# Attention and a bilinear feed-forward on one core: queries and keys by transposing DMAs, and the second tile's outputs by seven products

## The chip, the cores and the metric

The kernel runs on one core of a Trainium2 chip. The metric is the device time of one execution in microseconds (us), the median of three runs. A core has five engines that this text names as the profile does: PE (TensorE, matrix products; its weight loads are listed as PEld), DVE (VectorE), ACT (ScalarE), POOL (GpSimd) and SP (SyncE). Sixteen DMA engines move data between DRAM and on-chip memory. Here POOL issues the loads from DRAM (queue 0 in the profile) and SP the stores and on-chip copies (queue 1).

## The reference

Eight batches of attention with 8 heads, 576 positions and 64 features per head; then a feed-forward over all 4608 positions. The first four heads of a batch see only the last 32 positions ("local"), the last four only positions of the same remainder modulo 32 ("strided").

```python
def _attn_ref(q, k, v):
    scores = scale * np.matmul(q, k.transpose(0, 1, 3, 2))
    rel = pos[:, None] - pos[None, :]
    mask_local = (rel >= 0) & (rel < stride)                       # stride = 32
    mask_strided = (rel >= 0) & (pos[None, :] % stride == pos[:, None] % stride)
    ...
    attn = np.exp(scores)
    attn = attn / (np.sum(attn, axis=-1, keepdims=True) + 1e-09)
    return np.matmul(attn, v)

def _moe_ref(x, w_a, w_b, w_out):
    a = x @ w_a
    b = x @ w_b
    return a * b @ w_out
```

x is the attention's output with the heads side by side, 4608 x 512; w_a and w_b are 512 x 1536, w_out is 1536 x 512. All inputs and the output are float32 in DRAM; the kernel computes in bf16 with float32 sums.

## The kernel before, in words

**Work and order.** The feed-forward is cut into 9 tiles of 512 positions (t = 0 to 8). A tile has 16 slots: 12 slots `ffn_ab` (L629), each with the products of one block of 128 columns of w_a and w_b (eight matmuls of 512 columns, L626), a copy of the first result by ACT (L647) and the multiplication by DVE (L650, L652) into `pf`; then 4 slots for the outputs. Slot i of tile t is number 16 t + i. The attention of batch b is cut into small steps that are put between the matmuls of tile b - 1 by tables (`STEPS`, `LATER`, `IN_Y`, L584 to L592): S0 to S7 are scores (matmuls L392, exponential by ACT L413, mask by DVE L431), V0 to V7 the products with the values. A step at a half number lies in the middle of a slot. Every engine runs its instructions in the order in which the program records them, and waits at each for what it needs.

**An attention unit V** of the third batch (b = 2), and V4 to V7 of the later ones, is `step_VT` (L518): matmuls into the one bank pair `o` (L529), on ACT a logarithm and an exponential (L538, L539) that make reciprocals, and two multiplications by DVE (L543, L545) into `xT`, which free `o`.

**Outputs of a tile** come in two ways. The plain product, `ffn_y` (L886), has 48 matmuls of 512 columns (L892), four ACT copies (L901) and four stores. Tiles in `FAST_Y` use seven products in place of eight quarter products, `y_plan` (L815): sums of `pf` blocks are made before by DVE in `fast_s` (L754, L764) and of weights in `fast_w` (L172); then 7 x 2 x 6 = 84 matmuls of 256 columns (L830) go into three banks X, Y and Z in the order 1, 7, 6, 4, 5, 2, 3 (`Y_ORDER`, L803). Each bank collects several products, and each product's end is copied by ACT or added by DVE (`y_post`, L789, L795, L797, L799, L801) before the next product adds into the same bank. 21 matmuls make a slot, and a step in the middle of a slot comes after the 11th. Before the change `FAST_Y` holds tiles 2 to 8; tiles 0 and 1 use the plain product.

**Queries and keys of a batch.** The scores need keys (`kT_buf`) and queries (`qz_buf`) with the features on the partitions; the queries of two heads stand there twice, each time with the other head's half zero. Batches 0 and 1 are transposed by PE (`T_p`, L279). From the third batch on (`FIRST_D` = 2), `load_qk` (L187) brings keys and queries by POOL into on-chip tiles (`kl`, `ql` at L212, `natk`, `natq` at L203), `step_D` (L320) transposes blocks of 32 x 32 with DVE (L329, L334), and SP copies the pieces into place, 8 key copies (L346) and 16 query copies (L350) per batch. The zeros in the queries are written once (`zero_qz`, L114, and `rezero`, L355, on POOL at slot 14).

**What sets the times.** `do(i, ...)` (L1008) hangs loads, transposes and stores on slots. From slot 14 on, POOL first copies one element that the slot has produced (`pace`, L1076), so its loads are issued no earlier than that slot. SP has no such pace: a DMA on it starts as soon as the ones before it are issued and what it waits for is there. Local rows also use a transposing DMA already: `rows_out` (L508) writes the attention's result to DRAM (`xd`) and `rows_in` (L514, L516) reads it back transposed into `xT`, 576 rows of 128 columns at a time.

**The start.** SP loads the first heads (`raw`, L934 to L936) and POOL all the rest; the weights come in pieces (`load_w`, L249), then `wo_sb`, then the third batch's queries and keys at slots 0 and 1 of the program's order.

Of the kernel before, what the change touches and what calls it, by code (L numbers as in the profile page):

```python
# [8 lines left out]
BF16 = mybir.dt.bfloat16  # L9
# [5 lines left out]
FIRST_D = 2  # L15
RL = 6
RS = 8
NP = 72
GP = 80
NY = 18  # L20
YS = 24
# [5 lines left out]
FAST_Y = (2, 3, 4, 5, 6, 7, 8)  # L27
# [4 lines left out]
def kernel(  # L32
# [46 lines left out]
    qz_buf = [[tuple(t[:, j] for t in pair) for j in range(2)] for pair in qz_pair]  # L79
# [4 lines left out]
    nat_s = {nm: const.tile([128, 3, RS * D], BF16, name=f"nat{nm}") for nm in "qk"}  # L84
# [27 lines left out]
    spare = qz_buf[0][0][0][:, 0]  # L112

    def zero_qz(i, eng, parts=((0, 0), (0, 1), (1, 0), (1, 1))):  # L114
        for j, z in parts:
            t = qz_buf[i][j][z]
            if (i, j, z) == (0, 0, 0):
                t = t[:, 1]
            if eng is nc.scalar:
                nc.scalar.copy(t, spare[:, :1].unsqueeze(2).to_broadcast(list(t.shape)))  # L120
            else:
                eng.memset(t, 0.0)

# [63 lines left out]
    def load_qk(b, strided, heads=range(HL), names="kq"):  # L187
        for nm in names:
            src = {"k": k, "q": q}[nm]
            if b < FIRST_D:  # L190
                n, R, h0 = (NP, RS, HL) if strided else (96, RL, 0)
                w0 = {"k6": 0, "q6": 1536, "k8": 3072, "q8": 5120}[f"{nm}{R}"]
                if b not in shared:
                    shared[b] = nat.tile([128, FG * 5 * SW], BF16, tag="shared", name="shared")
                t = nats[b, nm, strided] = shared[b][:n, w0:w0 + HL * R * D].rearrange("p (h r d) -> p h r d", r=R, d=D)
                hs = slice(heads[0], heads[-1] + 1)
                nc.gpsimd.dma_start(out=t[:, hs], in_=src[b, h0:h0 + HL].rearrange("h (p r) d -> p h r d", r=R)[:, hs])  # L197
            elif strided:

                t = nat_s[nm]  # L200
                n = 32 if b == FIRST_D else YS
                for h in heads:
                    nc.gpsimd.dma_start(  # L203
                        out=t[32 * h:32 * h + n],
                        in_=bass.AP(tensor=src.tensor, offset=(b * H + HL + h) * S * D,
                                    ap=[[RS * D, n], [YS * RS * D, 3], [1, RS * D]]))
            else:
                if 0 in heads:
                    nats[b, nm, strided] = nat.tile([128, NY, D], BF16, tag=f"{nm}l", name=f"{nm}l")
                t = nats[b, nm, strided]  # L210
                for h in heads:
                    nc.gpsimd.dma_start(out=t[32 * h:32 * h + 32],  # L212
                                        in_=src[b, h].rearrange("(i y) d -> y i d", y=32))
            nats[b, nm, strided] = t
# [105 lines left out]
    def step_D(b, z, nm, part):  # L320
        src = nats.get((b, nm, z == 1))
        if part == 0:
            tl[b, z, nm] = blocks(nm, z)
        t = tl.get((b, z, nm))
        if part is None:
            last = True
        elif z == 0:
            i = slice(NY // 2 * part, NY // 2 * (part + 1))
            nc.vector.transpose(t.rearrange("p h (i y) -> p i h y", i=NY)[:, i],  # L329
                                src[:, i].rearrange("p i (h d) -> p i h d", h=2))  # L330
            last = part == 1
        else:

            nc.vector.transpose(  # L334
                t.rearrange("p h (r c) -> p r h c", r=RS)[:, :, :, YS * part:YS * part + 32],
                src[:, part].rearrange("p (r h d) -> p r h d", r=RS, h=2))
            last = part == 2
        if last:
            for nm, c in {"k": (("k", 0),), "q": (("q", 0), ("k", 1), ("q", 1)), "r": (("k", 1), ("q", 1))}[nm]:
                if part is not None and z == 1 and c == 1 and b > FIRST_D:  # L340
                    continue
                t = tl[b, z, nm]
                for e in range(2):
                    if nm == "k":
                        dst = kT_buf[b % 2][z][64 * e:64 * e + 64, c]
                        nc.sync.dma_start(out=dst[:, PAD:] if z == 0 else dst[:, :RS * GP], in_=t[64 * c:64 * c + 64, e])  # L346
                        continue
                    for j in range(2):
                        r0 = 64 * c + 32 * j
                        nc.sync.dma_start(out=qz_buf[b % 2][j][z][64 * e + 32 * j:64 * e + 32 * j + 32, c],  # L350
                                          in_=t[r0:r0 + 32, e])
                if (nm, c, z) == ("q", 0, 0) and b - 1 > FIRST_D:
                    rows_in(b - 1, 1)

    def rezero(b):  # L355

        for j in range(2):
            for t in qz_buf[b % 2][j]:
                nc.gpsimd.memset(t[32:64] if j == 0 else t[64:96], 0.0)
# [22 lines left out]
    def S_p(b, u):  # L382
        c, half, M, n, G = unit(u)
        kT = kT_buf[b % 2][c // 2]

        st = pst.tile([128, 2, 512], F32, tag="st", name="st")
        held[b, "st", u] = st
        if b > 0:
            sv = st.rearrange("p a (i n) -> p (a i) n", n=256)
            for i in range(G):  # L390
                k0 = (G * half + i) * (LW if c < 2 else GP)
                nc.tensor.matmul(sv[:, i, :2 * n].rearrange("p (j n) -> p j n", j=2), lhsT=kT[:, c % 2, k0:k0 + 128],  # L392
                                 rhs=qz_pair[b % 2][c // 2][:, :, c % 2, k0:k0 + n], start=True, stop=True)
            return
        qz = tl[0, c // 2, "q"]
        if b == 0 and c >= 2:
            for j in range(2):
                r = slice(64 * j, 64 * j + 64)
                nc.tensor.matmul(st[:, j, :W], lhsT=nm_l[r], rhs=nm_r[r].unsqueeze(1).to_broadcast([64, G, n]),
                                 start=True, stop=False)  # L400
        for i in range(G):
            k0 = (G * half + i) * (LW if c < 2 else GP)
            for j in range(2):
                d = slice(64 * j, 64 * j + 64)
                nc.tensor.matmul(st[:, j, i * n:(i + 1) * n], lhsT=kT[d, c % 2, k0:k0 + 128],
                                 rhs=qz[d, c % 2, k0:k0 + n], start=c < 2, stop=c < 2 or i == G - 1)
# [161 lines left out]
    def step_X(b, c):  # L568
# [16 lines left out]
                 10: "V6 Tk0", 10.5: "Tq0 Pk1 Z0", 11: "Pq1", 12: "V7 Tk1 S0 W0 W1", 12.5: "Tq1 W2",  # L585
                 12.6: "S1", 12.75: "L0 X2", 13: "s2 X3 V0 m2 L1 W3", 13.5: "V1 S3", 14: "V2 X0", 14.5: "V3 D1", 15: "X1"},
             2: {20: "S0", 20.5: "S1", 21.5: "V0", 22: "S2", 23: "V1", 23.5: "S3", 24.5: "V2", 25: "S4", 26: "V3", 26.5: "S5",
                 27.5: "V4", 28: "S6", 28.5: "V5", 29: "S7", 29.5: "V6", 30.5: "V7"}}
    LATER = {-1: "S0", 0: "S1", 1: "V0", 2: "S2", 3: "V1 O0", 4: "S3 I0", 5: "V2", 6: "S4", 7: "V3 O1", 8: "S5", 9: "V4",
# [5 lines left out]
          "Z": lambda b, n: zero_qz(0, nc.vector, ((1, 1),)), "D": lambda b, n: step_D(FIRST_D, 0, "k", n)}  # L595
# [325 lines left out]
    with tc.manual_schedule(engines={ENG.PE, ENG.SP, ENG.Pool, ENG.DVE, ENG.Activation}):  # L921
# [20 lines left out]
        zero_qz(1, nc.scalar, ((0, 1),))  # L942
# [9 lines left out]
        for nm in ORDER:  # L952
# [24 lines left out]
            elif nm == "Z":  # L977
                zero_qz(1, nc.scalar, ((0, 0),))
# [25 lines left out]
        steps[16 * (B - 2) + 9][-1][1].append("I1")  # L1004
# [16 lines left out]
        for b in range(FIRST_D, B):  # L1021
# [7 lines left out]
            else:  # L1029
                for h in range(HL):  # L1030
                    do(g0 + h + (2 if b == FIRST_D + 1 else -2), load_qk, b, False, (h,))
                    do(g0 + h + (6 if b == FIRST_D + 1 else 2), load_qk, b, True, (h,))
                    do(g0 + h + 10, load_vs, b, (h,))
                do(g0 + (10 if b == FIRST_D + 1 else 7), load_vl, b)
            gs = {2: (14, 14, 15, 15, 16, 16, 17, 17, 18, 18), 3: (8, 9, 10, 11, 12, 13, 14, 15, 16, 17)}.get(b) or (
                3, 5, 7, 9, 12, 13, 14, 15, 16, 17)
            for (z, nm, part), g in zip(((0, "k", 0), (0, "k", 1), (0, "q", 0), (0, "q", 1), (1, "k", 0), (1, "k", 1),
                                         (1, "k", 2), (1, "q", 0), (1, "q", 1), (1, "q", 2)), gs):
                if (b, z, nm, part) != (FIRST_D, 0, "k", 1):
                    do(g0 + g, step_D, b, z, nm, part)  # L1040
            if b > FIRST_D:
                do(g0 + 19, step_D, b, 1, "r", None)
# [9 lines left out]
        do(1, zero_qz, 1, nc.vector, ((1, 1),))  # L1052
        do(4, zero_qz, 1, nc.vector, ((1, 0),))
        for i, jz in ((2, (0, 0)), (3, (1, 0)), (0, (0, 1))):
            do(i, zero_qz, 0, nc.vector, (jz,))
        do(14, rezero, 1)
# [53 lines left out]
```

## Time and profile before

| what | value |
|---|---|
| median of 3 runs | 325.23 us (325.07 to 325.52) |
| span of the profiled execution, first to last instruction | 324.3 us |
| mean granted clock of PE | 0.999 |
| share of the chain that ended last: PE, DMA, POOL | 88%, 5%, 4% |
| DMA packets, amount | 110725, 40.44 MB |

The profile shows one execution. Its parts are: the busy time of each engine, the span in 40 slices, the DMA queues, the chain of work that ended last (followed back from the last instruction to what released it), the costliest groups of instructions, and the DMA issues. In a group's line stand the source line, engine and operation, output and input with their shapes, the count, the busy time and the mean of one in ns, and then the idle time of the engine before them with what ended it. In a timeline a line is: start, length, engine, source line, operation, shapes, count. Matmuls overlap in the pipeline, so their listed lengths (379 ns for 512 columns) are longer than the distance from one start to the next. The records of single DMA packets give start, length, size and queue.

### The profile page before, as it was taken

The numbers are of one execution on the slowest core, as the hardware profiler recorded it, in microseconds if no ns is written. First come the engines' busy times: TensorE is split into PE (matmuls) and PEld (weight loads), VectorE is DVE, ScalarE is ACT, GpSimd is POOL, SyncE is SP. The second block draws the span as 40 slices with busy tenths as digits, with TensorE's granted clock in tenths as the row PEclk, the third lists the DMA queues.
The fourth block names the chain that finished last, engine by engine and source line by source line (L and its number), as shares of the span: only waits on it lengthen the run. The fifth ranks groups of instructions, "written<-read, shape, count | busy, mean of one in ns | idle before, by whom it ended". The sixth has DMA issues, their size and how long they took to land.

```text
span 324.3 us, 7477 instructions
## 1 busy us (share of the span) xinstructions
PE 316.7 (98%) x2669; PEld 211.2 (65%) x2698; DVE 259.9 (80%) x563; ACT 190.9 (59%) x338; POOL 162.7 (50%) x293
## 2 busy tenths in 40 slices
PE   8999999999999999999999999999999999999994
PEld 7764555455555577556999895559555866786684
DVE  6766797888878988898889888988999667857862
ACT  6762776468674576447654765467546655535541
POOL 8844938689948534762576338734004003202520
PEclk9999999999999999999999999999999999999999
DMA  8999999899999999999899999999137030004004
GB/s 154 138 203 195 203 191 173 169 173 143 133 224 124 147 88 99 107 187 179 94 111 183 183 108 92 158 205 131 30 81 166 20 115 18 0 2 129 1 3 129
DMA packets 110725, 40.44 MB, mean 125 GB/s; under 512 B 88672, under 2 KB 107744, under 8 KB 110688
## 3 DMA queue, kind: packets, MB, share of 16 engines
q0 software_dynamic: 85968, 19.48, 66.0%
q1 hardware_dynamic: 24576, 20.42, 24.9%
q8 instruction: 21, 0.34, 0.4%
q14 instruction: 16, 0.13, 0.1%
q10 hardware_dynamic: 144, 0.07, 0.1%
HBM read 39.51 MB, written 10.91 MB: 155 GB/s over the span
## 4 chain that ended last, share of the span: by engine, by line
PE 88%; DMA 5%; POOL 4%; DVE 1%; issue 1%; ACT 1%; POOLq 0%
PE mm L626 42%; PE mm L830 17%; PE mm L892 6%; PE mm L710 5%; DMA wb_sb<-in_moe_w_b_dram 5%; PE st L392 4%; PE ax L703 3%; PE mm L703 2%; PE o L529 2%; PE o L470 2%; PE mm L857 2%; POOL shared L197 1%; PE end L857 1%; POOL wa_sb L252 1%; POOL vl L225 1%
## 5 line engine op out<-in xcount | busy, mean ns | idle before, releaser
L626 PE MATMUL mm<-xT,wb_sb 128*128 128x512 bf16 (+1 forms) x381 | 88.2, 352 | 0.7 <-DMA wb_sb<-in_moe_w_b_dram 0.4
L626 PE MATMUL mm<-xT,wa_sb 128*128 128x512 bf16 (+1 forms) x367 | 86.6, 351 | 0.8
L647 ACT COPY a_sb<-mm 128x512 f32<-128x512 f32 x84 | 49.2, 586 | 47.6 <-PE mm L626 45.6
L626 PEld LDWEIGHTS <-wb_sb 128*128 128x128 bf16 x392 | 37.8, 98 | 34.3 <-DMA wb_sb<-in_moe_w_b_dram 1.1
L1076 POOL CAST pace<-pf 1x1 f32<-1x1 bf16 x82 | 24.5, 298 | 64.3 <-DVE pf L650 42.7
L626 PEld LDWEIGHTS <-wa_sb 128*128 128x128 bf16 x392 | 35.1, 98 | 21.1
L650 DVE TENSOR_TENSOR pf<-a_sb,mm 128x512 bf16<-128x512 f32 x62 | 42.1, 679 | 7.3 <-PE mm L626 6.1
L413 ACT ACTIVATE p<-st 72x576 bf16<-72x576 f32 (+1 forms) x56 | 36.4, 650 | 14.4 <-PE st L392 14.2
L545 DVE TENSOR_TENSOR xT<-o,xr 64x288 bf16<-64x288 f32 x48 | 21.4, 446 | 14.8 <-ACT xr L539 14.5
L830 PEld LDWEIGHTS <-ps 128*128 128x128 bf16 x288 | 28.0, 98 | 3.1
L795 ACT COPY y_sb<-mm 128x512 f32<-128x512 f32 (+1 forms) x28 | 15.6, 556 | 17.6 <-PE mm L830 15.0
L830 PE MATMUL mm<-wf,ps 128*128 128x256 bf16 x216 | 25.5, 273 | 0.0
L710 PE MATMUL mm<-xT,wb_sb 128*128 128x512 bf16 x83 | 25.3, 379 | 0.1
L538 ACT ACTIVATE xr<-o 64x576 f32<-64x576 f32 x28 | 18.1, 648 | 12.1 <-PE o L529 11.9
L892 PE MATMUL mm<-wo_sb,pf 128*128 128x512 bf16 x93 | 23.1, 379 | 0.2
L243 POOL DMA_DIRECT2D vs<-in_v_dram x24 | 19.7, 820 | 4.8 <-PE mm L830 2.4
L830 PEld LDWEIGHTS <-pf 128*128 128x128 bf16 x216 | 20.3, 98 | 2.5 <-issue 0.2
L1076 POOL COPY pace<-y_sb 1x1 f32<-1x1 f32 x23 | 4.6, 200 | 33.1 <-DVE y_sb L793 20.1
L539 ACT ACTIVATE xr<-xr 64x576 f32<-64x576 f32 x28 | 19.1, 683 | 0.9
L652 DVE TENSOR_TENSOR pf<-a_sb,mm 128x512 bf16<-128x512 f32 x22 | 14.9, 677 | 4.8 <-ACT a_sb L647 2.7
L212 POOL DMA_DIRECT2D kl<-in_k_dram x24 | 16.0, 667 | 5.2 <-issue 2.9
L830 PE MATMUL mm<-wo_sb,pf 128*128 128x256 bf16 x144 | 18.5, 273 | 0.1
(189 smaller groups left out, 598.0 us busy)
## 6 DMA issues: line engine op xcount, KB each, us to landing
out_dram<-y_sb SPq DMA_DIRECT2D x12, 512.0 KB, 4.8
out_dram<-y_sb SPq DMA_DIRECT2D x11, 256.0 KB, 3.9
vl<-in_v_dram POOLq DMA_DIRECT2D x6, 384.0 KB, 7.8
kl<-in_k_dram POOLq DMA_DIRECT2D x24, 72.0 KB, 3.1
ql<-in_q_dram POOLq DMA_DIRECT2D x24, 72.0 KB, 3.2
vs<-in_v_dram POOLq DMA_DIRECT2D x24, 72.0 KB, 4.3
wo_sb<-in_moe_w_out_dram POOLq DMA_DIRECT2D x4, 384.0 KB, 9.5
natk<-in_k_dram POOLq DMA_DIRECT2D x20, 72.0 KB, 3.6
```

The source lines that it names most:

```text
L243: nc.gpsimd.dma_start(out=vs_buf[b % 2][:, h, :, 0:D], in_=v[b, HL + h].rearrange("(p r) d -> p r d", r=RS))
L413: nc.scalar.activation(p_flat(p)[:M, :2 * W].rearrange("p (i n) -> p i n", n=2 * n), st[:M].rearrange("p a (i n) -> p (a i) n", n=256)[:, ...
L538: nc.scalar.activation(r, sums, ACT.Ln)
L539: nc.scalar.activation(r, r, ACT.Exp, scale=-1.0)
L545: nc.vector.tensor_mul(dst.rearrange("d (p r) -> d p r", r=RS)[:, :, G * half:G * (half + 1)], o[:64, j, :W].rearrange("d (g p) -> d p g", ...
L626: nc.tensor.matmul(ps_[:, c0:c0 + n], lhsT=w[:, kk, 128 * f:128 * (f + 1)], rhs=xT[:, kk, x0:x0 + n], start=(kk == first and c0 == 0), sto ...
L647: nc.scalar.copy(a_sb, ab[0])
L650: nc.vector.tensor_mul(pf[:, f, :].rearrange("p (i a s) -> p a i s", i=2, s=16), halves(a_sb), halves(ab[1]))
L710: nc.tensor.matmul(got[e], lhsT=wb_sb[:, kk, 128 * f:128 * (f + 1)], rhs=xT[:, kk, x0:x0 + TTOK], start=kk == 0, stop=kk == KD - 1)
L830: nc.tensor.matmul(bank[b][:, q], lhsT=lhs(g, q), rhs=rhs(g), start=k in "172" and q == 0 and g == 0, stop=g == FG - 1, skip_group_check=True)
L892: nc.tensor.matmul(ybank[j], lhsT=pf[:, f, 128 * j:128 * (j + 1)], rhs=wo_sb[:, f], start=(f == 0), stop=(f == FD - 1))
L1076: nc.gpsimd.tensor_copy(pace, done)
```

## The change

Three things change together.

- From the third batch on, `load_qk` writes keys and queries, converted to bf16, into DRAM tiles (`kr0`/`kr1` for keys with two buffers each, `q_rows` for queries with one each), and `step_D` reads them with transposing DMAs on SP: per batch and kind of head one for the keys (576 rows of 256 columns) and four for the queries (576 rows of 128 columns). DVE's transposes and the 24 copies per batch are gone.
- The zeros stand in the DRAM rows beside each query: `zero_rows` writes them once for each kind, by SP from a tile `spare`. `rezero` on POOL and part of `zero_qz` are gone. The order of the recorded program leaves the two zeroing DMAs with one wait, for DVE's first memset, and directly behind the three `raw` loads on SP.
- `FAST_Y` takes tile 1 in, so its outputs are made by `y_plan`, with `fast_s` on DVE before.

The core of the diff:

```diff
-FAST_Y = (2, 3, 4, 5, 6, 7, 8)
+FAST_Y = (1, 2, 3, 4, 5, 6, 7, 8)
...
-    qz_buf = [[tuple(t[:, j] for t in pair) for j in range(2)] for pair in qz_pair]
+    qz_buf = [[tuple(t[:, :, j] for t in pair) for j in range(2)] for pair in qz_pair]
+    q_rows = [dram.tile([S, HL, 2, D], BF16, name=f"qr{z}", tag=f"qr{z}", bufs=1) for z in range(2)]
...
-    spare = qz_buf[0][0][0][:, 0]
+    spare = const.tile([96, FD * D], BF16, name="spare")
...
+    def zero_rows(z):
+        nc.sync.dma_start(out=q_rows[z].rearrange("(p g) (c j) e d -> p (g c) (j e d)", g=6, j=2)[:, :, D:2 * D],
+                          in_=spare.rearrange("p (n d) -> p n d", d=D))
...
+            if (b, nm, strided) not in nats:
+                nats[b, nm, strided] = q_rows[strided] if nm == "q" else dram.tile([S, HL, D], BF16, tag=f"kr{strided}",
+                                                                                  name=f"kr{strided}")
+            rows = nats[b, nm, strided]
+            if nm == "q":
+                rows = rows[:, :, 0]
+            if strided:
+
                 for h in heads:
+                    nc.gpsimd.dma_start(out=rows[:, h].rearrange("(r p) d -> p r d", r=RS),
+                                        in_=src[b, HL + h].rearrange("(p r) d -> p r d", r=RS))
             else:
+                nc.gpsimd.dma_start(out=rows, in_=src[b, :HL].rearrange("h t d -> t h d"))
...
+    def step_D(b, z, nm, c=None):
+
+        rows = nats[b, nm, z == 1]
+        if nm == "k":
+            t = kT_buf[b % 2][z]
+            nc.sync.dma_start(out=t[:, :, PAD:] if z == 0 else t[:, :, :S], in_=rows.rearrange("t h d -> t (h d)"),
+                              transpose=True)
+            return
+        flat = rows.rearrange("t h e d -> t (h e d)")
         for j in range(2):
+            nc.sync.dma_start(out=qz_pair[b % 2][z][:, c, j, :S], in_=flat[:, 256 * c + D * j:256 * c + D * j + 128],
+                              transpose=True)
...
+                do(18 if b == FIRST_D + 1 else g0 - 2, load_qk, b, False)
                 for h in range(HL):
-                    do(g0 + h + (2 if b == FIRST_D + 1 else -2), load_qk, b, False, (h,))
                     do(g0 + h + (6 if b == FIRST_D + 1 else 2), load_qk, b, True, (h,))
...
+            gs = {2: (15, 15, 15, 18, 18, 18), 3: (9, 10, 11, 14, 15, 16)}.get(b) or (5, 6, 7, 10, 11, 12)
+            for (z, nm, c), g in zip(((0, "k", 0), (0, "q", 0), (0, "q", 1), (1, "k", 0), (1, "q", 0), (1, "q", 1)), gs):
+                do(g0 + g, step_D, b, z, nm, c)
...
-        do(14, rezero, 1)
+        do(10, zero_rows, 0)
+        do(11, zero_rows, 1)
```

In the last lines g0 is 16 (b - 2). The strided scores of the later batches now step by 72 columns instead of 80, and the second half of the local result (`rows_in(b, 1)`) is issued from the table `LATER` at position 9 instead of from `step_D`.

## The prediction

> **What bounds the kernel now.** I read the page first (busy shares and chain), then PE's waits, then the timelines at the three places that the change touches. Busy shares and the chain:
>
> ```profile
> PE 316.7 (98%) x2669; PEld 211.2 (65%) x2698; DVE 259.9 (80%) x563; ACT 190.9 (59%) x338; POOL 162.7 (50%) x293
> ...
> PE 88%; DMA 5%; POOL 4%; DVE 1%; issue 1%; ACT 1%; POOLq 0%
> ```
>
> PE is busy in 98% of the span and makes 88% of the chain. All that PE waited for by name, in the whole execution:
>
> ```profile
> PE misc L155 <- PEq L1094: 0.9, 1, 0.9
> PE mm L626 <- DMA wb_sb<-in_moe_w_b_dram: 0.4, 1, 0.4
> PE tp L296 <- DMA shared<-in_q_dram: 0.3, 1, 0.3
> ```
>
> Nothing is on this list after 29.1 us, where the third piece of `wb_sb` lands. From 57 to 317 us the matmul starts follow each other at 216 ns for 512 columns (8 in 1.73 us in the chain) and 109 ns for 256 (12 in 1.31 us); the few larger gaps, about 0.2 us each, are single records missing from the trace. So after 57 us every matmul taken away is a gain, every stall put in is a loss, and DVE's 80% costs nothing today.
>
> **The change part by part.** The sum is made against the profiled span, 324.3 us; the median of the runs, 325.2, lies 0.9 above it, and I keep that.
>
> 1. *Second tile, plain product to seven products.* Out go 48 matmuls of 512 columns: 48 x 0.2163 = 10.38 us. In come 7 x 2 x 6 = 84 of 256 columns: 84 x 0.1092 = 9.17 us. All lie on PE: **-1.21**.
>
> 2. *What the seven products wait for there.* In the third tile the phase begins with this on ACT:
>
> ```profile
> 117.01 0.65 ACT L538 ACTIVATE xr<-o 64x576 f32<-64x576 f32 x1 [0.54 <-PE o L529]
> 117.69 0.68 ACT L539 ACTIVATE xr<-xr 64x576 f32<-64x576 f32 x1
> 118.40 0.59 ACT L795 COPY y_sb<-mm 128x512 f32<-128x512 f32 x1
> 118.88 0.65 ACT L413 ACTIVATE p<-st 72x576 bf16<-72x576 f32 x1
> 119.88 0.59 ACT L795 COPY y_sb<-mm 128x512 f32<-128x512 f32 x1 [0.35 <-PE mm L830]
> ```
>
> The reader is to see that an attention unit V puts two ACT instructions (its logarithm starts 0.46 us after V does, then 0.65 + 0.68) ahead of the copy of product 1, and that product 6 adds into the bank that this copy reads. In the third tile one V stands ahead of the phase and two lie late in it. In the second tile four lie inside (V4 to V7 at positions 27.5, 28.5, 29.5, 30.5), with the scores S6 and S7. Counted from the first product matmul: V4 comes after 11 matmuls, at 1.20; ACT is through its pair at 3.03 and through copy 1 at 3.64. PE has product 1, V4 (0.25), product 7 and S6 (0.25) done at 3.12, so product 6 waits 0.5. The same count carried on: copy 6 stands behind V5's pair and ends at 6.94 where product 5 could start at 6.76 (0.2); copy 5 stands behind V6's pair and holds product 3 (0.14); V7 needs the bank that V6's two DVE multiplications free (0.1). Behind a waiting matmul everything on PE queues. Together **+0.9**, bounds 0 (copies always in time) and 1.5 (every V a full 0.5 late).
>
> 3. *The transposes leave DVE.* 60 stream transposes go (24 of 0.77, 36 of 0.70 us: 43.7 us), and POOL's four memsets at L359 (4.4 us). DVE gets ten sums for tile 1 (nine of 0.4, one of 0.66) and three additions of 0.68: +6.3. PE waits for DVE nowhere today: **0**.
>
> 4. *Zero rows.* Two new DMAs stand on SP behind the first three loads and wait only for DVE's first memset, over at 1.25 us, so they issue at about 2.2 us, not at slots 10 and 11 where the code has them. They write 2 x 1152 pieces of 128 bytes, 144 per DMA engine. Nothing like them is in the trace. The packet records give neighbours with 256-byte pieces: a transpose alone runs at 17.5 ns apiece per engine (458 starts in 0.5 us at 252.0), a write to DRAM at 24 (333 in 0.5 us at 111.5). So 2.5 to 3.5 us of every engine, from 4.6 us on, shared with the loads. Those set the start:
>
> ```profile
> 14.49 14.60 DMA wb_sb<-in_moe_w_b_dram
> 29.09 0.05 issue
> 29.14 1.90 PE mm L626 x8
> ```
>
> PE already stands still for 0.4 us before 29.14, so what delays this landing shows in full. Between 9 and 15 us POOL's issues, 0.7 to 0.8 us each, leave the engines about a fifth free, some 2 us, which hides most. I take **+0.5**; bounds 0 and 2.5.
>
> 5. *Third batch, the first through DRAM.* Its loads keep their place on POOL behind the weights. Local keys and queries keep 2304 descriptors each; strided ones go from 768 packets of 1024 bytes to 4608 of 128. Back to back the records show 600 starts of 128-byte packets per 0.5 us (at 48 us) against 100 of 1024 (at 43 us), so 3.8 us either way; they are in by about 58. SP then stands where it stands today:
>
> ```profile
> 57.90 1.77 SPq L346 DMA_DIRECT2D kT0l<-tk  x2
> 59.78 0.53 SPq L903 DMA_DIRECT2D out_dram<-y_sb  x1
> 60.40 2.48 SPq L350 DMA_DIRECT2D qz0l<-tq  x4
> ```
>
> The fourth store now issues at 58.25 (its copy ends then), the key transposes at 58.8. One 576x128 piece costs SP 1.15 us when nothing holds it and lands 2.4 us after its issue begins (both from the existing transpose at L516; behind a large store it issued in 2.84). Keys are two pieces, the first chunk's queries two: issued by 63.4, landed by 64.7, or 65.6 behind the store. The first score needs them here:
>
> ```profile
> 66.36 0.41 PE L392 MATMUL st<-qz0l,kT0l 128*128 128x192 bf16 x3
> ...
> 69.48 0.42 PE L529 MATMUL o<-p,vl 128*128 128x96 bf16 x6
> ```
>
> About 1 us is left. The values `vl` that the second row needs (issued 61.34, landed 67.8 today) now share the engines with transposes that take 36 x 17.5 = 630 ns of each 1150: 192 packets per engine at 13.3 ns become some 5.7 us instead of 3.5, landing near 70. **+0.35**; bounds 0 and 2. POOL's second load of queries waits, the buffer being single, until the third batch's query transposes have read it, near 68; behind it stand the pace copies and `vs`, which V4 needs at 82.3 and which still issues by 76: 0.
>
> 6. *Later batches.* Per batch SP issues 12 pieces x 1.15 = 13.8 us against 24 copies x 0.59 = 14.2, in a tile of 34 us. Engine time: 12 x 0.63 = 7.6 us in, 24 copies (1024 packets at 60 ns, 3.8 us) out, strided loads 3.8 for 2.9: today's packets of a tile at these prices come to about 20 us, after it to 25, of 34. The local keys are issued at slots 5 to 7 of a tile for scores at slot 15, the strided at 10 to 12 for 22: **0**.
>
> Sum: -1.21 + 0.9 + 0.5 + 0.35 = +0.55, so 325.2 + 0.55 = **325.8**. Less than 0.2% (0.65 us), about what a measurement of this kernel can tell from no change, lies between 324.6 and 325.9; the forecast is at the upper edge.
>
> Two rules of the Trainium skill speak against the change. "VectorE: DVE Perf Modes" (The three transpose paths) gives a 128x128 block 311 ns on VectorE and 1309 by DMA; by it a piece of 4.5 blocks would be an estimated 5.9 us, 12 of them 71 us in a tile of 34, and the sum would be some 180 us worse. The trace shows 1.15 us per piece, so I give that little weight. "DMA: Bandwidth & Descriptors" (Specifications) says that below 512 bytes a transfer is a read-modify-write; the 256-byte writes at 24 ns against 17.5 fit a small surcharge, and no run here shows 128-byte ones.
>
> **The rivals.**
> - *The gain comes through.* ACT's copies are in time or the zero rows fit in the gaps: at least 0.65 of the 1.75 us of costs is absent. For it: PE waits for ACT nowhere today. Against it: ACT's program order in the second tile. 324.0 to 324.7. Chance 0.16.
> - *The third batch comes late: slower.* Place: first score at 66.36. If a 128-byte packet into DRAM costs 26 ns instead of 13.3, 9216 of them take 15 us, not 7.7: the strided queries land at 65 and `vl`, in the same queue behind them, near 71.5; with pieces held to 1.8 us, between 1.15 and 2.84, four issue by 66 and land at 67.3. PE then stands 2 us in place of 0.35; with -1.21 + 0.9 + 0.5 of parts 1, 2 and 4 that is 325.2 + 2.2 = 327.4. It decides once keys and queries land more than 1 us later than counted. For it: a margin of 1 us. Against it: queue 0 is nearly empty at 58 us. Chance 0.22.
> - *SP becomes the bound: slower.* If every later piece issues in 2.84 us, 12 make 34 us, with 4.3 for the other issues 38 in a tile of 34: 4.5 us x 5 tiles, 348. Against it: that row stands only behind 512 KB stores. This is where the first rule above would lead, only further. Chance 0.06.
>
> **How the numbers follow.** Forecast 0.52, its own range 325.0 to 326.6: 0.32 within 0.2%, 0.20 slower. First rival 0.13 faster, 0.03 within. The other two 0.28 slower. The last 0.04 I halve between faster and slower. Faster 0.15, same 0.35, slower 0.50. The range 324.4 to 328.2 leaves out the best end of the first rival and SP as the bound.
>
> **What would show it.** Part 1: 84 rows of 256 columns at tile 1. Part 2: gaps before product 6 of 0.5 us with ACT's copy as releaser. Part 4: two issues at 2.2 us on SP, and `wb_sb`'s landing later than 29.1. Part 5: a wait of L364 or L501 for DMA near 66 to 70. Wrong would be waits for transposes after 100 us, or no gap in tile 1.

## The result, and the profile after

The changed kernel takes **330.22 us** (median of four runs, 327.28 to 331.36), the kernel before beside it 325.38 us (325.07 to 325.77). The ratio is 1.0136, with a 95% interval of 1.009 to 1.0183: slower by about 4.5 us, where I had forecast 325.8 and a range up to 328.2. Its runs lie 4 us apart, those of the kernel before 0.7 us. The comparisons below leave out executions that were slow at a lower granted clock; of the changed kernel's repetition, after_again, that leaves one of four.

The profiled execution took 330.83 us with a span of 329.1 us, 4.8 us over that of before. The page of the changed kernel, busy shares and chain:

```profile
PE 317.7 (97%) x2734; PEld 214.6 (65%) x2734; DVE 230.5 (70%) x513; ACT 191.5 (58%) x339; POOL 154.6 (47%) x236
...
PE 77%; DMA 15%; ACT 3%; POOL 2%; DVE 1%; issue 1%; POOLq 0%; ACTq 0%
```

DVE is busy for 29 us less; its records, which overlap, are 36 us shorter in sum, where 37 were counted. But the DMA share of the chain goes from 5% to 15%. What PE waited for in the changed kernel (total us, times, longest):

```profile
PE mm L598 <- DMA xT<-xd: 3.2, 2, 1.8
PE o L442 <- DMA vl<-in_v_dram: 0.9, 2, 0.5
...
PE mm L802 <- ACT y_sb L767: 0.4, 1, 0.4
```

The first line is new. L598 is the feed-forward's matmul (L626 before), and it waits for `xT<-xd`: the transposing DMA of `rows_in` (L488, was L516), a part of the kernel whose amount of work the change leaves as it was (it moves only the place from which the second half's read-back is issued). The chain of waits of the changed kernel at that place:

```profile
183.21 8.25 DMA xd<-xl
191.48 6.66 DMA xT<-xd
198.18 1.02 PE mm L598 x4
```

The local result of two heads is written to DRAM (8.25 us to land), read back transposed (6.66 us), and PE stands still until 198.18. In the kernel before the same two steps took 6.53 and 4.87 us and ended 2.3 us before PE needed them. Where the 4.8 us went, from the starts of the matmul records at the first product of each tile:

| stretch | before, us | after, us | difference |
|---|---|---|---|
| start to second tile | 57.70 | 58.50 | +0.80 |
| second tile | 35.63 | 35.30 | -0.33 |
| third and fourth tile | 67.34 | 67.63 | +0.29 (a gap of 0.30 at 128.1, at the same matmul) |
| fifth tile | 34.18 | 33.91 | -0.27 (a gap at 184 us of before is absent) |
| sixth tile | 33.67 | 35.65 | **+1.98** (the wait above) |
| seventh tile | 33.42 | 34.97 | **+1.55** (the same wait at 231.6) |
| eighth tile to last matmul | 57.80 | 57.80 | 0 |
| last matmul to end | 4.60 | 5.37 | +0.77 (the last store landed 3.5 us after its issue instead of 2.5) |

The last row I take for chance: among all the profiles below that store lands now after 2.5, now after 3.5 us. The rest is two facts: a start 0.8 us later, and 3.8 us of waits for the row outputs.

The DMA side shows them coming. From the stages 162 to 196 us of the kernel before and of the changed one (after the length of the stage: busy time of PE, PEld, DVE, ACT, POOL, then the granted clock, DMA share, GB/s; the share is the sum of packet times over 16 engines' time, so packets in flight together count twice):

```profile
162.00:196.00 34.00, 33.84 (x355) 30.21 (x354) 29.40 (x61) 20.18 (x33) 18.70 (x36) 1.00 1.10 141
```

```profile
162.00:196.00 34.00, 34.00 (x361) 30.52 (x359) 24.05 (x51) 20.27 (x34) 18.35 (x28) 1.00 1.82 150
```

1.10 became 1.82, with hardly more bytes per second. The share does not say how full the engines are: back to back, 128-byte loads alone show 2.46 (changed kernel, 49 us), transposes alone 1.05 (kernel before, 252 us). The packet records of these stages: 9924 of 128 bytes before, 14592 after; 2304 of 256 bytes before (the expectation of packed_loads has 1152), some 8300 to 10000 after in the three later stages.

The packet records show one thing more. Twice in the trip above the engines of the changed kernel move next to nothing, for 1.2 us in the write and for 1.4 us in the read-back (the last two numbers are the DMA share and GB/s):

```profile
184.10:185.30 1.20, 1.20 (x19) 1.10 (x18) 1.17 (x4) 0.59 (x1) 0.37 (x1) 1.00 0.70 12
195.90:196.60 0.70, 0.47 (x3) 0.10 (x1) 0.60 (x2) 0.54 (x1) 0.19 (x1) 1.00 0.00 0
196.60:197.30 0.70, 0.00 (x0) 0.00 (x0) 0.33 (x1) 0.00 (x0) 0.00 (x0) 1.00 0.09 9
```

Just ahead of each, at 183.6 and 195.0 us, a packet of 16 KB starts on queue 8 (instructions) and takes 1.0 and 1.7 us; in the kernel before such a packet, at 184.0, passes while the engines move 192 GB/s. Packets of up to 512 bytes that take over 0.7 us number 366 in the changed kernel and 161 to 419 in the other kernels below that send keys or queries through DRAM, but 23 in the kernel before and 26 in seven_only, which send neither. These stops last 2.6 us in the two legs, which together are 3.5 us longer than before. They are not the whole: in no_q_transposes the same two legs are 0.9 and 0.5 us longer than before without one. No run takes the stops away and leaves the transfers, so what makes them and what they cost is not shown.

### The profile page after: what moved, and what is told of

Its sections match the earlier page's. It is cut to its first block, busy times and chain, and to the rows that moved or that the text cites. A ratio compares the mean times of both kernels' runs of the same rounds, so it can differ in the third digit from the quotient of the medians.

```text
span 329.1 us, 7287 instructions
## 1 busy us (share of the span) xinstructions
PE 317.7 (97%) x2734; PEld 214.6 (65%) x2734; DVE 230.5 (70%) x513; ACT 191.5 (58%) x339; POOL 154.6 (47%) x236
## 4 chain that ended last, share of the span: by engine, by line
PE 77%; DMA 15%; ACT 3%; POOL 2%; DVE 1%; issue 1%; POOLq 0%; ACTq 0%
PE mm L598 40%; PE mm L802 11%; DMA xd<-xl 7%; DMA xT<-xd 6%; PE mm L682 6%; PE st L364 3%; PE mm L864 3%; PE ax L675 3%; PE o L442 2%; DMA vl<-in_v_dram 2%; PE mm L675 2%; PE mm L829 2%; PE o L501 2%; POOL shared L199 1%; PE end L829 1%
## 5 line engine op out<-in xcount | busy, mean ns | idle before, releaser
L598 PE MATMUL mm<-xT,wa_sb 128*128 128x512 bf16 (+1 forms) x384 | 88.5, 352 | 3.3 <-DMA xT<-xd 3.2
L598 PE MATMUL mm<-xT,wb_sb 128*128 128x512 bf16 (+1 forms) x384 | 88.5, 352 | 0.0
L622 DVE TENSOR_TENSOR pf<-a_sb,mm 128x512 bf16<-128x512 f32 x74 | 50.7, 685 | 29.7 <-PE mm L598 18.8
L598 PEld LDWEIGHTS <-wb_sb 128*128 128x128 bf16 x392 | 37.9, 98 | 37.7 <-issue 4.6
L1041 POOL CAST pace<-pf 1x1 f32<-1x1 bf16 x72 | 24.1, 335 | 75.6 <-DVE pf L622 60.5
L598 PEld LDWEIGHTS <-wa_sb 128*128 128x128 bf16 x392 | 35.1, 98 | 21.2
L802 PEld LDWEIGHTS <-ps 128*128 128x128 bf16 x336 | 32.4, 98 | 4.5 <-issue 1.0
L802 PE MATMUL mm<-wf,ps 128*128 128x256 bf16 x252 | 30.4, 273 | 0.5 <-ACT y_sb L767 0.4
L767 ACT COPY y_sb<-mm 128x512 f32<-128x512 f32 (+1 forms) x32 | 17.9, 560 | 17.5 <-PE mm L802 14.7
L802 PEld LDWEIGHTS <-pf 128*128 128x128 bf16 x252 | 23.7, 98 | 2.9
L211 POOL DMA_DIRECT2D krTrue<-in_k_dram x24 | 20.6, 901 | 3.6 <-issue 2.0
L211 POOL DMA_DIRECT2D qr<-in_q_dram x24 | 19.5, 813 | 5.4 <-DMA wo_sb<-in_moe_w_out_dram 1.2
L802 PE MATMUL mm<-wo_sb,pf 128*128 128x256 bf16 x168 | 21.7, 273 | 0.0
L736 DVE TENSOR_TENSOR ps<-pf 128x512 bf16<-128x512 bf16 (+1 forms) x49 | 19.7, 402 | 0.8
```

The lines of the kernel that those rows point to most:

```text
L211: nc.gpsimd.dma_start(out=rows[:, h].rearrange("(r p) d -> p r d", r=RS), in_=src[b, HL + h].rearrange("(p r) d -> p r d", r=RS))
L598: nc.tensor.matmul(ps_[:, c0:c0 + n], lhsT=w[:, kk, 128 * f:128 * (f + 1)], rhs=xT[:, kk, x0:x0 + n], start=(kk == first and c0 == 0), sto ...
L622: nc.vector.tensor_mul(pf[:, f, :].rearrange("p (i a s) -> p a i s", i=2, s=16), halves(a_sb), halves(ab[1]))
L736: nc.vector.tensor_tensor(s[:, n], a, b, op=op)
L802: nc.tensor.matmul(bank[b][:, q], lhsT=lhs(g, q), rhs=rhs(g), start=k in "172" and q == 0 and g == 0, stop=g == FG - 1, skip_group_check=True)
L1041: nc.gpsimd.tensor_copy(pace, done)
```

## The experiments

"Waits" are gaps between matmul starts in the profiled execution, beyond the length of the matmul.

### The change taken apart

**seven_only**: only the second tile's seven products, in the kernel before.

```diff
-FAST_Y = (2, 3, 4, 5, 6, 7, 8)
+FAST_Y = (1, 2, 3, 4, 5, 6, 7, 8)
```

> The kernel before, with the second tile's outputs by seven products and nothing else: VectorE's stream transposes and the copies on SP stay. The two parts of my sum that belong here are -1.21 us of matmuls and +0.9 us of waits for ACT (1.05 us in the profile of the changed kernel), so 0.2 to 0.3 us faster than before, about 325.1, with PE gaps near 85, 88 and 91.5 us. A rival: VectorE, which keeps the transposes here, cannot take the second tile's sums and additions in time, and the phase stalls for DVE: then 326 or more.

Measured 327.05 us, ratio 1.005 (1.0033 to 1.0067): slower by 1.6 us, the rival. PE in the second tile (L529 is V):

```profile
82.42 0.42 PE L529 MATMUL o<-p,vs 72*128 72x72 bf16 x8 [0.33 <-DVE xT L543]
...
86.82 0.37 PE L529 MATMUL o<-p,vs 72*128 72x72 bf16 x6 [0.88 <-DVE xT L545]
```

The four gaps of part 2 are there as counted (0.55, 0.23, 0.15, 0.13), and two more for DVE (0.49 and 1.04): with the transposes still on it DVE is busy for 31.4 of the 34 us from 58 to 92 (24.1 in the changed kernel) and frees the bank too late. So the two halves of the change belong together: the way through DRAM is what makes the second tile's products worth 0.3 us instead of costing 1.

**path_only**: the other part alone, `FAST_Y` without tile 1.

> The changed kernel with the second tile by the plain product again, so only the way through DRAM and the transposing DMAs is left. If the loss is all in that way (row outputs late at two or three tiles, zero rows at the start), this is as slow as the changed kernel or 0.2 us slower: 330.0 to 330.5, and PE again waits for the row outputs' transposes near 196 and 231 us. If the second tile's seven products shift the later tiles into the collision, the waits go and it comes near 326.5.

Ratio 1.0076 (1.0054 to 1.0099; 327.8 and 328.6 us). One wait for the row outputs, 2.3 us at 229; that at 196 was absent. The waits belong to the way through DRAM, and which tile they hit changes from run to run.

**keys_only**: keys through DRAM, queries by DVE as before, second tile by seven products.

> One part of the change alone: keys through DRAM and transposing DMAs, queries by VectorE's transposes and copies as before, the second tile by seven products. DMA share per tile between 1.1 and 1.7, near 1.35. If lateness needs nearly full engines, the row outputs are in time and there is no wait after 100 us; the start has no zero rows (0.4 us less); VectorE has half its relief, so the second tile's two waits for DVE (1.5 us where VectorE keeps all transposes) are between 0 and 1.0: 325.2 to 326.5 by this. If instead the order on SP is the cause, the row outputs wait for the key pieces and it is 327 or more.

325.88 us, ratio 1.0011 (0.9999 to 1.0024). Shares per tile 1.39, 1.33, 1.22, no wait for a DMA after 100 us, in the second tile one wait for DVE of 0.73. All as expected. This part of the load costs nothing that these runs can tell.

### The start

**zeros_late**: zero rows behind a DVE instruction of slot 1.

```diff
-        do(10, zero_rows, 0)
-        do(11, zero_rows, 1)
+        do(1, nc.vector.memset, spare[:, :1], 0.0)
+        do(2, zero_rows, 0)
+        do(2, zero_rows, 1)
```

> The changed kernel with the two writes of zero rows held back by a small VectorE memset in slot 1 (near 22 us) in place of 2.2 us. Theory that they cost the start: the first batch's waits for vl (0.63 and 0.60 us at 11.1 and 14.9 us) go and it is 1.0 to 1.5 us faster than the changed kernel. If the start is slower for another reason, or the delay only moves to the weights and the second batch's loads, no change within 0.4 us.

Ratio 1.0095 (1.0061 to 1.0129), 0.4% under the changed kernel's 1.0136, with overlapping intervals. The waits for `vl` shrink, others come at 38.6, 41.4 and 54.1 us (0.28, 0.22, 0.18). Over all profiles here the second tile begins at 57.5 in the three kernels without zero rows and at 58.2 in the mean of twelve that write them early: 0.7 us. In the two that write them late it begins at 58.0 and 58.9 (early_both, below), so moving them does not remove it.

### Is it SP's order or the engines?

**rows_first**: the local query transposes behind the row outputs.

```diff
-            gs = {2: (15, 15, 15, 18, 18, 18), 3: (9, 10, 11, 14, 15, 16)}.get(b) or (5, 6, 7, 10, 11, 12)
+            gs = {2: (15, 15, 15, 18, 18, 18), 3: (9, 10, 11, 14, 15, 16)}.get(b) or (5, 9, 10, 11, 12, 13)
```

> The changed kernel with the local query transposes of the fifth batch on moved from positions 6 and 7 of a tile to 9 and 10, behind the row outputs' own transposes on SP, and the strided ones one position later. Theory of the order (the row outputs' writes and transposes stand behind four query pieces in SP's queue): the waits near 128, 196 and 231 us go, 3.5 to 4 us less than the changed kernel in the same execution, 326.3 to 326.8. Theory of the full engines (the 128-byte loads in GpSimd's queue make every transfer land late, whatever SP's order): the row outputs still land 6 us after their issue and PE still waits 2 us or more, 328 or more.

329.95 us, ratio 1.0135 (1.012 to 1.015): nothing gained. But the names changed. PE's waits in rows_first:

```profile
PE st L364 <- DMA qz0l<-qr: 1.5, 2, 1.1
PE st L364 <- DMA qz1l<-qr: 1.4, 2, 0.8
```

The row outputs now come 7 us early near 196 us and the queries, which stand behind them, late at all four tiles: 0.55, 0.77, 1.27 and 0.94 us, 3.5 in all, nearly as much as the three waits before (3.8). SP's queue shows the reason:

```profile
181.18 0.58 SPq L483 DMA_DIRECT2D xd<-xl  x1
187.28 1.16 SPq L488 DMA_TRANSPOSE xT<-xd  x1
188.53 5.14 SPq L330 DMA_TRANSPOSE qz0l<-qr  x4
```

SP waits 5.5 us at the instruction that needs the write landed, and the queries queue behind it. The theory that order alone was the loss falls.

**packed_loads** and **no_q_transposes**: each takes away one kind of the added packets. The first writes contiguous pieces to DRAM:

```diff
-                    nc.gpsimd.dma_start(out=rows[:, h].rearrange("(r p) d -> p r d", r=RS),
-                                        in_=src[b, HL + h].rearrange("(p r) d -> p r d", r=RS))
+                nc.gpsimd.dma_start(out=flat[n * h:n * (h + 1)].rearrange("(p m) -> p m", m=RS * D),
+                                    in_=x.rearrange("(p r) d -> p (r d)", r=RS))
```

The second returns from `step_D` ahead of the query transposes for `b > FIRST_D + 1`.

> The changed kernel with the loads of queries and keys from the third batch on written to DRAM as contiguous pieces of 1024 bytes, in the order of the input, and the zero rows as pieces of 1536; the queries and keys that the scores then read are in the wrong order, and the number of DMAs, their bytes and all transposes are the same. Theory of the full engines, with the small packets as the cause (14592 packets of 128 bytes per tile against 9924 before): the row outputs' transposes land in time again, no wait near 196 and 231 us, DMA share per tile from 1.7 to 1.3 or less, 3 us or more faster than the changed kernel, 326 to 327. Rival, the transposes as the cause (8064 packets of 256 bytes per tile against 1152): the row outputs still land 6 us after their issue and PE still waits 1 us or more, 328 or more.

> The changed kernel without the transposes of the queries from the fifth batch on (its scores use old queries); all loads stay. Eight of a tile's ten issues of transposes on SP for queries and keys go, with 4608 packets of 256 bytes. Theory of the transposes as the cause: row outputs land 3.5 to 4.5 us after their issue as before the change, the waits go, 326 to 327. Theory of the small load packets: the waits shrink little, 328 or more.

In both profiles no wait for a DMA after 100 us. packed_loads and no_q_transposes from 162 to 196 us:

```profile
162.00:196.00 34.00, 34.00 (x363) 30.86 (x361) 23.95 (x50) 20.27 (x34) 11.96 (x28) 1.00 1.27 159
```

```profile
162.00:196.00 34.00, 33.95 (x357) 30.24 (x356) 24.04 (x51) 20.16 (x33) 18.32 (x28) 1.00 1.34 122
```

So in these profiles neither the small loads nor the transposes are the cause by themselves; either kind alone leaves room, both together do not. no_q_transposes takes 325.72 us (1.0017, 1.0 to 1.0034). packed_loads is still at 329.93 (1.0135, 1.0113 to 1.0156), against my expectation: its profiled execution lost 1 us at the start, 2.0 in waits for the third batch's values and queries (0.81 and 0.34 at 70 to 72, 0.83 at 98.5) and 1.0 by the last store. For this kernel the time does not confirm what the profile shows of the later tiles.

**after_again, local_early, between, early_both**: the changed kernel once more, and three other orders: local transposes at positions 3, 4, 5; at 5, 8, 9; at 3, 4, 5 with the late zero rows.

> The changed kernel once more, beside the three below. All theories: 329 to 331 us, with waits for the row outputs' transposes in the tiles near 196 and 231 us.

> The changed kernel with the local key and query transposes of the fifth batch on at positions 3, 4 and 5 of a tile in place of 5, 6 and 7, so that SP's queue is empty of them when the row outputs of position 7 are written; the same transfers otherwise. The two theories that the runs so far leave: (1) the DMA engines are so full (share 1.7 per tile) that whatever comes last is late, so the waits stay or move to the queries: 328.5 or more; (2) each transfer lands 2 to 4 us later than before, but there is room in the tile, and the loss is in what was put where: the row outputs are written at once (near 13.9 us ahead of the tile's first use, as before the change), land in under 6 and 5.5 us, and the queries too are in time. Then no wait after 100 us, 3 to 3.5 us less than the changed kernel, 326.3 to 327.

> The changed kernel with one pair of local query transposes between the row outputs' write and their transpose (position 8) and the other pair behind it (position 9); with both pairs behind (the earlier run), SP stood idle 5.5 us for the landing of the write and the queries were 0.6 to 1.3 us late. By theory (2) the pair fills that time, the last pair is 2.5 us earlier and in time, and the row outputs too: within 0.5 us of the early placement. By theory (1) one of the two is still late by 1 us or more per tile: 328 or more.

> The early placement together with the late zero rows (VectorE memset in slot 1). If the start's cost is the zero rows, 0.5 us less than the early placement alone, and by theory (2) 325.8 to 326.5 in all; less than the kernel before only if the start costs nothing and the second tile's 0.2 us come through.

| kernel | us | ratio (95%) | waits for row outputs, us |
|---|---|---|---|
| after_again | 327.46 (one execution; the profiled one took 332.96) | - | 3.05, 0.59, 1.21 |
| local_early | 327.32 | 1.0049 (1.0028 to 1.007) | 1.10 |
| between | 327.93 | 1.0056 (1.0035 to 1.0077) | 1.87 |
| early_both | 327.24 | 1.0024 (0.9987 to 1.0062) | 1.18, 0.92 |

Against the changed kernel's first ratio, 1.0136, order helps by 0.8 to 1.1% (the last with the late zero rows); the one execution of after_again that is compared here took no longer than they did. Of the changed kernel's eight executions six took 329.6 us or more, of these three kernels' 27 one. Order heals nothing: a wait stays in each profile. In local_early the write of the row outputs still took 7.7 us with no transpose issued behind it; three query pieces and `vl` were still under way when it was issued. My theory (2), room enough if only the order is right, is refuted as I put it.

### Is the mix dearer, or is a stretch too full?

**probe**: transposes alone, strided loads alone, and both at once, added where the engines are idle.

> The changed kernel with idle-time probes added in the eighth tile, where its DMA engines are nearly empty: four query transposes alone (near 274 us), eight strided loads to DRAM alone (near 279 us), and both at once (near 288 us), into tiles that nothing reads. Alone I expect 576 packets of 256 bytes per 1.25 us of issue (35 ns per packet and engine as issued, 17.5 at best) and 600 packets of 128 bytes per 0.5 us at best, but limited here by the issue, 0.81 us for 576. If the mix is dearer than its parts, the transposes of the third probe land 2 us or more later after their issue than those of the first, or the packets of both together take over 1.3 times the sum; if not, both land as alone, within 1 us.

Landing of the four added transposes (L1037) in the first and the third stretch, us from issue, least, median, most:

```profile
DMA to landing us min/median/max: 2.7/3.5/3.9
```

```profile
DMA to landing us min/median/max: 3.4/5.1/5.4
```

The loads went from a median of 3.4 to 5.1. So with both under way a transfer lands about 1.6 us later: less than my mark for a dearer mix (2 us), more than my mark for none (1 us). My other mark, 1.3 times the sum of the prices, cannot decide. Between 298 and 305 us, with both under way, the records count 3171 packets of 128 and 2290 of 256 bytes. At the best prices alone (13.3 and 17.5 ns, from the prediction) that is 82 us of engine time, 5.1 us on each of 16 engines, and it took 7, 1.37 times as much. But alone, too, the transposes took 5.5 us for packets worth 2.5 (2304 of 256 bytes), and the loads 7.1 us for packets worth 3.8 (4608 of 128): the issue alone takes 5.1 us for the four pieces on SP and 6.4 for the eight loads on POOL, by themselves and together. In the fullest half microseconds of the mix, at 301.5, 303.0 and 304.5, the packets reach 0.9 of what the prices allow. That a mix is dearer than its parts is not shown, nor that the engines of a tile were full.

**vs_late**: only the loads of strided values moved, from position 10 to 15; SP's order is the changed kernel's.

```diff
-                    do(g0 + h + 10, load_vs, b, (h,))
+                    do(g0 + h + (10 if b == FIRST_D + 1 else 15), load_vs, b, (h,))
```

> The changed kernel with the loads of strided values vs from the fifth batch on at position 15 in place of 10, behind the next batch's local loads; SP's order is the changed kernel's. If the load of the engines in the stretch of the row outputs is what makes them late, the write lands in 7 us in place of 8.3 and the transpose in 5.5 in place of 6.7, and the waits near 128, 196 and 231 us shrink from 2 us to 0.5 or nothing: 327.5 or less. If only SP's order counts, they stay: 329 or more.

327.21 us, ratio 1.0071 (1.0039 to 1.0103). Everything that PE waited for in vs_late:

```profile
PE misc L157 <- PEq L1059: 0.9, 1, 0.9
PE tp L287 <- DVE tq L276: 0.7, 1, 0.7
PE o L442 <- DMA vl<-in_v_dram: 0.5, 1, 0.5
PE mm L802 <- ACT y_sb L767: 0.4, 1, 0.4
```

No wait for a DMA after the second tile, although the share per tile is as high as ever (1.66, 1.72, 1.78) and SP's order is unchanged. The write landed in 5.5 us and the transpose in 4.3. So here it counted in which stretch a transfer stands, not how many a tile has. Three of its ten executions took 330 to 332 us; they may have waits that this profile cannot show.

**early_vs_late**: local_early and vs_late together.

> The early placement of the local transposes together with the late vs. By both causes together the last wait for the row outputs (1.1 us in the profile of the early placement) goes: 326.0 to 326.6, that is the kernel before plus the start's 0.5 us and minus the second tile's 0.2. If the early placement's remaining wait is of another kind, no change from 327.3.

330.95 us, ratio 1.016 (1.0145 to 1.0175): the expectation fails. `vs` now travels at 164 to 178 us, beside the transposes that local_early moved there; the write of the row outputs takes 7.8 to 9.4 us from the fifth tile on, and waits of 0.56 and 2.0 us are back (0.7 more for the third batch's values, and the start 1.9 us later than before). Two moves, each good alone, are bad together; that they fill the same gap is argued from these rows.

**copies_on_dve** tests step 2: the second tile's copies of products 1, 6, 5 and 3 by DVE instead of ACT.

> The changed kernel with the second tile's copies of products 1, 6, 5 and 3 on VectorE in place of ACT. By my step 2 the gaps there are ACT's order: those before product 6 (0.56 us) and at 88.5 and 91.6 us go, about 0.9 us less in that tile (35.30 us from its first matmul to the third tile's in the changed kernel, 34.4 here). If VectorE is late in its turn, gaps of the same size with DVE as the releaser. The waits for the row outputs stay.

331.82 us, ratio 1.0199 (1.0149 to 1.025). PE's wait in the second tile (those for the row outputs stay):

```profile
PE mm L802 <- DVE y_sb L767: 3.6, 3, 1.5
```

The gaps turn into 1.6, 1.3 and 1.2 us with DVE as the releaser. DVE had time in sum (70% busy), not at that moment.

The row outputs' trip at the tile near 196 us, in all of these:

| kernel | write issued | lands in | transpose lands in | ahead of PE's need |
|---|---|---|---|---|
| before | 182.0 | 6.5 | 4.9 | 2.3 |
| changed | 183.2 | 8.2 | 6.7 | -1.9 |
| rows_first | 181.2 | 6.1 | 3.9 | 7.2 (queries late) |
| local_early | 185.6 | 7.7 | 4.0 | -1.1 |
| packed_loads | 183.7 | 6.9 | 6.7 | 0.7 |
| no_q_transposes | 180.2 | 7.4 | 5.4 | 2.6 |
| keys_only | 180.6 | 7.0 | 5.0 | 3.1 |
| vs_late | 184.8 | 5.5 | 4.3 | 1.5 |

None of these kernels beats the kernel before.

## Why the prediction was wrong

**The step that failed is part 6**, "Later batches: 0". It asked whether the moved keys and queries would be in time, and they were. It did not ask about the row outputs, which use the same queue and the same engines and whose amount the change does not touch. They had 2.3 us to spare; the write was issued 0.7 us later against the sixth tile's start and the two legs became 1.7 and 1.8 us longer (the read-back was issued 0.02 us after the write had landed, so its new place in the program held nothing up). That is 3.8 us in the profiled execution where the sum has 0. That the added transfers are what makes the legs longer is shown by the shorter legs when a part of them is taken away or moved (no_q_transposes, keys_only, vs_late; one profile each); by what means they do it is open. "Waits for transposes after 100 us" stood in the prediction as what would make it wrong; they came, for another tile than those I had in mind.

Its second mistake is in the same part: the 13.8 us of SP and the 25 of 34 us of the engines are averages over a tile, where by vs_late the stretch counts. SP's issues of keys and queries (L325, L330) took 18 to 20 us in each of the three later stages. SP's queue shows the stretch in the changed kernel, with issues of 4.06 us for one piece and 5.96 us for two, where a piece needs 1.1 to 1.4 when nothing holds it:

```profile
176.13 4.06 SPq L325 DMA_TRANSPOSE kT0l<-krFalse  x1
180.29 2.83 SPq L330 DMA_TRANSPOSE qz0l<-qr  x2
183.21 0.54 SPq L483 DMA_DIRECT2D xd<-xl  x1
183.81 5.96 SPq L330 DMA_TRANSPOSE qz0l<-qr  x2
```

The rest, step by step:

1. *Seven products, -1.21, and 2. their waits, +0.9.* Right: gaps of 0.56, 0.23, 0.15 and 0.12 us where 0.5, 0.2, 0.14 and 0.1 were counted, and the tile as a whole -0.33 for -0.31. ACT of the changed kernel, V4's pair ahead of the copy of product 1:

```profile
83.43 0.65 ACT L510 ACTIVATE xr<-o 64x576 f32<-64x576 f32 x1 [0.94 <-PE o L501]
84.11 0.68 ACT L511 ACTIVATE xr<-xr 64x576 f32<-64x576 f32 x1
84.82 0.59 ACT L767 COPY y_sb<-mm 128x512 f32<-128x512 f32 x1
```

3. *DVE's relief, 0.* Right in size. But without it the tile's sums would have cost 1.5 us of waits for DVE, by seven_only, which I had not seen; and PE did wait for DVE once in the kernel before, 0.27 us at 184 us, which is gone (the fifth tile of the table).
4. *Zero rows, +0.5.* 0.8 in the profile, 0.7 in the mean. The place was wrong, so the near size is luck: `wb_sb` landed at 28.76, earlier than before, and PE waited instead for `vl`, whose first piece landed at 11.8 instead of 10.0. That the zero rows are the cause is argued from these landings; zeros_late did not settle it.
5. *Third batch, +0.35.* No wait in the profiled execution: keys landed at 63.2, the first queries at 65.2, `vl` at 70.0 as counted. In seven other profiles there is a gap of 0.1 to 0.8 us ahead of V0, in three of them with `vl`, the transfer that I had named, as the releaser.

Of the rivals, the gain, the third batch late by 2 us and SP as the bound did not happen: SP's issues became longer, as said, but did not fill the tile. The Trainium skill's 1309 ns by DMA for a 128x128 block ("VectorE: DVE Perf Modes", The three transpose paths) does not carry over to these pieces: four pieces of 4.5 blocks, 18 blocks, landed within 7.2 us in the probe. The Trainium skill's read-modify-write below 512 bytes ("DMA: Bandwidth & Descriptors", Specifications) does not show in the rate either: 128-byte packets into DRAM start 1200 times per us at 49 us, as many as into on-chip memory before the change.

What stays open: through what the added transfers make the others land later, and how much of it is the stops of all engines; why one execution of the changed kernel takes 327.3 and another 333.6 us, beyond that the late tiles differ (the kernel before, too, took 329.7 us once in the 22 executions beside after_again); and how much of the start is the zero rows.

## What to carry to other kernels

When a change adds DMAs to a queue, list every other transfer of that queue and of the engines with its slack, those first that make two trips in a row (written, waited for, read back): they pay twice for every slower landing. A mean of engine time over a stage hides the stretch that decides. If moving one transfer makes another late by the same amount, move load out of the stretch and check what already stands where it goes. Before a mix is called dearer than its parts, measure the parts in the same way.

## What the runs showed of the hardware

**A wait of 3 us costs more than itself.** In after_again the row outputs were 2.9 us late at the fourth tile. PE then:

```profile
131.21 0.59 PE L598 MATMUL mm<-xT,wa_sb 128*128 128x512 bf16 x1 [2.89 <-DMA xT<-xd]
131.59 0.63 PE L598 MATMUL mm<-xT,wb_sb 128*128 128x512 bf16 x1
132.02 0.63 PE L598 MATMUL mm<-xT,wa_sb 128*128 128x512 bf16 x1
```

The starts are 0.43 us apart where 0.216 is usual, for 2.5 us, and the granted clock of the stage is 0.95: the clock records have half the clock from 130.4 to 133.8 us. In the probe a wait of 3.5 us for DVE, ending at 289.8, was followed by 3.4 us at half the clock in the same way. After gaps of 1.97 us (changed kernel) and 2.27 (path_only) the next matmuls ran at 0.216, and between the first 7 us and the last matmul the clock records of all 17 profiles show no other fall. So the kernel's own wait lowered the clock in these two executions; what it does in those without a profile is not known. The Trainium skill says that the clock falls to half after an idle window of about 3.4 us, which runs freely ("TensorE: Matmul & The Clock Gate", Part 1); here a wait of 2.9 us, shorter than that window, was enough.

**Transfers of two queues on the same engines land later together**, by about 1.6 us in the probe, transposes (3.5 to 5.1) and loads (3.4 to 5.1) alike. The Trainium skill says that each engine goes round between the queues packet by packet ("DMA: Bandwidth & Descriptors", Queues, rings and completion order); by that both get shares, as both did here.

**The last store** lands after 2.5 or after 3.5 us, nothing between: 3.5 in 5 of 17 profiles, in no visible relation to the kernel.
